# A fused attention and MLP kernel: first loads on one GpSimd queue, a new opening, a halved last tile

## The chip, the cores and the metric

The kernel runs on one core of one Trainium2 chip. The metric is the device time of one launch in microseconds (us), lower is better. Engines are named as in the profile: PE (TensorE matmul), PEld (its weight load), DVE (VectorE), ACT (ScalarE), POOL (GpSimd) and SP (SyncE, which only issues DMAs here).

## The reference

A linear attention with decay over 768 positions (4 batches, 8 heads, head size 64) is followed by an MLP with a "snake" activation. In the reference the attention goes block by block:

```python
intra = np.einsum('bhic,bhjc->bhij', qb, kb) * Dmask[None]
intra = np.einsum('bhij,bhjd->bhid', intra, vb)
inter = np.einsum('bhid,bhde->bhie', qb * lam_pow[None], kv_state)
out[:, :, sl] = intra + inter
kv_state = lam_block[None, :, None, None] * kv_state + np.einsum('bhsd,bhse->bhde', kb_dec, vb)
...
h = x @ w_in                       # x: 3072 x 512, w_in: 512 x 2048
s = np.sin(alpha * h)
g = h + s * s / (alpha + 1e-09)
return (g @ w_out)                 # w_out: 2048 x 512
```

## The kernel before, in words

Work is recorded as a list of operations, each with an engine, a duration that the author assumed, and the buffers that it reads and writes. A planner (`Program.add`) gives every operation a start from these durations; `emit` sorts by start and adds the semaphore waits. So the order on each engine follows from the order of recording and from the assumed durations, and each engine executes its list strictly in that order. DMAs that convert float32 to bf16 (k, q, w_in as `w1`, w_out as `w2`) are issued by POOL, plain ones (v in float32, and the output) by SP.

**Attention.** A *step* s is half of a load block: load block d is 128 positions of a pair of batches with all eight heads, brought in by two DMAs each of k, q and v (one per batch of the pair, `u`), and step 2d takes heads 0 to 3, step 2d+1 heads 4 to 7. A step has three parts, all in `sec`: `t` transposes q and k (32 small PE transposes, then one copy `qkT` out of PSUM by DVE or ACT), `s` forms the scores (`S_m`: 16 PE matmuls and one DVE multiplication with the mask), and `o` forms output and state (PE reads `S_m`, the scaled `v2`, `qkT` and the state `Zs`; DVE scales the result into `xT`, and the state goes on through `Zacc` and `Zs`). `prep_v` multiplies v by its decay before `o` may use it.

**MLP.** Chunk c is 512 tokens, the output of steps 4c to 4c+3. `grp_A(c, m)` is one of 16 groups of four 128x512 matmuls with `w1` (then a sine on ACT, a square on POOL, ACT or DVE, and one DVE operation into `gT`). `grp_B(c, s4, m4)` is a quarter of the 16 matmuls with `w2` for output tile s4. The six chunks go through A, then B, and the attention steps of the next chunk stand between the B groups (`B0_SEC`, `SEC1`, `SEC`). A of a chunk needs all four of its steps.

**Loads at the start.** Steps 0 to 3 (load blocks 0 and 1) come before A of chunk 0; load blocks 2 and 3 (steps 4 to 7) must be there during B of chunk 0. Four w2 blocks of four `m` each and the v loads hang together by gates: v of load block 2 may be issued by SP only when the second w2 block has landed, v of block 3 only when the third has:

```python
ISSUE_A0 = {0: lambda: w2_next(0), 2: lambda: load(2, "k"), 4: lambda: load(2, "q"), 6: lambda: w2_next(1),
            8: lambda: load(2, "v", after=[gates[1]]), 9: lambda: load(3, "k"), 12: lambda: load(3, "q"),
            14: lambda: w2_next(2)}
```

Of the kernel before, what the change touches and what calls it, by code (L numbers as in the profile page):

```python
# [27 lines left out]
class Program:  # L28
# [57 lines left out]
    def add(self, eng, fn, dur, reads=(), writes=(), slot=None, nbytes=0, after=()):  # L86
# [20 lines left out]
        op.start = self.place(eng, max(t, self.issued[eng]), self.ISSUE[eng])  # L107
# [79 lines left out]
def bass_lightning_attn__then__act_snake_kernel(  # L187
# [31 lines left out]
    with es:  # L219
# [77 lines left out]
        def load(d, x, after=(), us=(0, 1)):  # L297
            pair, n = d // NB, d % NB
            r = d % RL
            src, dst = {"k": (k, k2), "q": (q, q2), "v": (v, v32)}[x]  # L300
            for u in us:
                a = bass.AP(src.tensor, (2 * pair + u) * H * S * D + n * BL * D, [[2 * D, 64], [S * D, H], [1, 2 * D]])
                op = rec("SP" if x == "v" else "POOL", lambda e, u=u, a=a: e.dma_start(dst[r][half(u), :, :], a), 0,  # L303
                         writes=[f"{x}.{r}.{u}"], slot=f"{x}{r}", nbytes=262144 if x == "v" else 131072, after=after)
            return op

        def consts():
# [26 lines left out]
        def consts3():  # L334
# [66 lines left out]
        def prep_v(s, engs=("POOL", "DVE")):  # L401
# [4 lines left out]
            reads, writes = [f"v.{r}.0", f"v.{r}.1", "Lv"], [f"v2.{c}"]  # L406
# [9 lines left out]
        def part_keys(x, s):  # L416
            return [f"{x}.{s // 2 % RL}.{u}" for u in range(2)]
        def sec(t=None, o=None, s=None, tb=None, sb_=S_BK, ob=O_BK, peek=False, t_engs=("DVE", "ACT"), via=None):
# [125 lines left out]
            if s is not None:  # L544
# [10 lines left out]
            if has_Z:  # L555
# [3 lines left out]
                if no == 0 and o > 1:  # L559
                    rec("ACT", lambda e: e.copy(zs, z), 0.37, reads=keys_o, writes=[f"Zs.{o % 3}"])  # L560
            if o is not None:
                x, col = (o // 4) % NX, 256 * (no % 2)
                xo = xT[x][:, 2 * ho:2 * ho + 2, col:col + 256].rearrange("p a (u i) -> p u a i", u=2)
                xi = PS[:, ob:ob + 2, 0:256].rearrange("p u (a i) -> p u a i", a=2)
                X_b = bass.AP(Xt, (2 * ho * NB + no) * 128, [[HS * NB * 128, 128], [0, 2], [NB * 128, 2], [1, 128]])
                rec("DVE", lambda e: e.tensor_tensor(xo, xi, X_b, ALU.mult), 0.72,  # L566
                    reads=keys_o + [f"X.{2 * ho + a}.{no}" for a in range(2)],
                    writes=[f"x.{x}.{o % 4}"])
            if o in (0, 1):
                rec("ACT", lambda e: e.copy(zs, z), 0.37, reads=keys_o, writes=[f"Zs.{o % 3}"])  # L570
            if has_Z:
                if no == 0:
                    rec("ACT", lambda e: e.copy(acc[:, :, :], z), 0.4, reads=keys_o, writes=[f"Zacc.{ho}"])
                else:
# [3 lines left out]
                        reads=[f"Zacc.{ho}"], writes=[f"Zs.{o % 3}"])  # L578
            if t is not None:
# [106 lines left out]
        prep_v(3, ("DVE",))
        w1_block(8, 8, after=[v1])
        sec(o=2, ob=4)
        sec(o=3, ob=6)
        alpha_ops(0)  # L690
        alpha_ops2()
        decay_table(2, NB)
        sin_table()
# [13 lines left out]
        def steady(i, peek=False):  # L707
# [4 lines left out]
            return sec(t=t, o=o, s=s, tb=(b, b), peek=peek)  # L712

        gates = {}

        def w2_next(j):
            gates[j] = w2_block(4 * j, 4)

        ISSUE_A0 = {0: lambda: w2_next(0), 2: lambda: load(2, "k"), 4: lambda: load(2, "q"), 6: lambda: w2_next(1),
                    8: lambda: load(2, "v", after=[gates[1]]), 9: lambda: load(3, "k"), 12: lambda: load(3, "q"),  # L720
                    14: lambda: w2_next(2)}

        def v_last():
            gates["v"] = load(3, "v", after=[gates[2]])

        def next_kq(d):
            load(d, "k", after=[gates["v"]])
            load(d, "q", after=[gates["v"]])

        ISSUE_B0 = {0: lambda: w2_next(3), 1: v_last, 9: lambda: next_kq(4)}  # L730
        ISSUE_A1 = {0: lambda: load(5, "k"), 3: lambda: load(5, "q"), 8: lambda: ahead(8), 11: lambda: ahead(9),
                    14: lambda: ahead(10)}
        every, low = range(8), range(4)
        B0_SEC = {3: dict(t=4, tb=(6, 7)), 5: dict(t=5, s=4, tb=(6, 6)), 7: dict(t=6, s=5, tb=(7, 7)),
                  9: dict(t=7, s=6, tb=(6, 6)), 10: dict(o=4, s=7, ob=6), 11: dict(o=5, ob=4),
                  12: dict(o=6, ob=6), 13: dict(o=7, t=8, tb=(6, 6), ob=4)}
        SEC = {2: 0, 5: 1, 8: 2, 10: 3}
        SEC1 = {4: 0, 6: 1, 9: 2, 11: 3}
        SQ = {3: "ACT", 6: "DVE", 8: "ACT", 11: "DVE", 13: "ACT"}
        for c in range(NCH):  # L740
            if c == 1:
                load(4, "v")
                load(5, "v")
            for m in range(NM):
                grp_A(c, m, every if m < 12 else range(2, 4) if m == 15 and c else range(4, 8),
                      (SQ.get(m, "POOL"),) if c > 1 else ("POOL", "ACT", "DVE"))
                if c == 0 and m in ISSUE_A0:
                    ISSUE_A0[m]()
                if c == 1 and m in ISSUE_A1:
                    ISSUE_A1[m]()  # L750
                if c == 1 and m == 7 or c > 1 and m in (3, 7, 11):
                    grp_B(c - 1, 3, 3 if c == 1 else m // 4 + 1, low)
            b_seq = [(s4, m4) for m4 in range(4) for s4 in range(2)] + [(2, m4) for m4 in range(4)] + [(3, 0)]
            if c == 0:
                b_seq = [(s4, m4) for m4 in range(2) for s4 in range(4)]
                b_seq += [(s4, m4) for s4 in range(3) for m4 in (2, 3)] + [(3, 2)]
            for i, (s4, m4) in enumerate(b_seq):
                if c == 0 and i in ISSUE_B0:
                    ISSUE_B0[i]()
# [46 lines left out]
```

## Time and profile before

| | |
|---|---|
| median of 3 runs | 239.6 us (239.52 to 240.24) |
| the profiled execution | 239.02 us, of which 237.2 us span |
| PE busy, share of the span | 213.8 us, 90% |
| DVE, ACT, POOL busy | 141.6, 124.1, 112.3 us |
| mean granted TensorE clock | 0.968 of full |
| data moved by the DMA engines | 23.49 MB, mean 99 GB/s |

The span runs from the first to the last instruction on the core; the 1.8 us between it and the device time are launch and end. Busy shares are averages over stages with different limits, so the stages have to be read one by one. The granted clock is the share of full TensorE speed that the chip allowed; full is 2.4 GHz, and 0.50 in a stretch means 1.2 GHz throughout.

### The profile page before, as it was taken

Reading aid. Unit: us, or ns where it says so; the run is one execution under the profiler, and the core shown is the slowest. Engines: PE = TensorE matmul, PEld = TensorE weight load, DVE = VectorE, ACT = ScalarE, POOL = GpSimd, SP = SyncE. Lnnn points to the kernel's source line nnn. Section 1 sums busy time; section 2 is a strip of 40 time slices with the busy share of each in tenths; the row PEclk is TensorE's granted clock in tenths of the full one; section 3 lists DMA queues with packets and bytes.
Section 4 is the critical chain, followed back from the end, with each engine's and each line's share of the span. In section 5 each row is a group of like instructions: output and inputs, shape, how many; then the busy total and the mean of one; then the engine's idle time right before and its main releaser. Section 6 shows DMA issues by size and latency. Waiting matters only on the chain.

```text
span 237.2 us, 6413 instructions
## 1 busy us (share of the span) xinstructions
PE 213.8 (90%) x2817; PEld 108.4 (46%) x2817; DVE 141.6 (60%) x202; ACT 124.1 (52%) x193; POOL 112.3 (47%) x146
## 2 busy tenths in 40 slices
PE   6355999569899999989999999999999999999993
PEld 5253344234444445544455544456444464444441
DVE  2647599043839995737875647865558756378300
ACT  3752599012049963357755367815377631668120
POOL 8568900081173562858554495553275600455300
PEclk9997699958999999999999999999999999999998
DMA  7999999939289990993052990222110203102033
GB/s 67 162 204 154 199 191 194 233 51 89 68 122 184 234 175 5 147 197 57 8 128 22 235 146 3 71 64 68 44 28 0 48 3 91 45 0 47 0 88 88
DMA packets 46283, 23.49 MB, mean 99 GB/s; under 512 B 26784, under 2 KB 42672, under 8 KB 46256
## 3 DMA queue, kind: packets, MB, share of 16 engines
q0 software_dynamic: 29568, 10.49, 38.8%
q1 hardware_dynamic: 16512, 12.59, 22.5%
q8 instruction: 22, 0.36, 0.7%
q14 instruction: 5, 0.04, 0.1%
q10 hardware_dynamic: 176, 0.01, 0.0%
HBM read 27.28 MB, written 6.29 MB: 142 GB/s over the span
## 4 chain that ended last, share of the span: by engine, by line
PE 64%; DMA 14%; DVE 11%; POOL 5%; ACT 3%; issue 1%; SPq 1%; POOLq 0%; ACTq 0%
PE PS L642 28%; PE PS L605 24%; DMA v<-in_v_dram 7%; DMA w<-in_moe_w_out_dram 5%; PE PS L429 4%; DVE S_m L553 4%; DVE gT L619 2%; DMA k<-in_k_dram 2%; PE PS L438 2%; ACT t L609 2%; PE PS L461 2%; PE PS L451 2%; DVE u L617 2%; POOL k L303 1%; DVE xT L566 1%
## 5 line engine op out<-in xcount | busy, mean ns | idle before, releaser
L642 PE MATMUL PS<-w,gT 128*128 128x512 bf16 x384 | 92.0, 385 | 0.0
L605 PE MATMUL PS<-xT,w 128*128 128x512 bf16 x384 | 88.3, 386 | 1.5 <-DVE xT L566 1.5
L619 DVE SCALAR_TENSOR_TENSOR gT<-u,r_sb,PS 128x512 bf16<-128x512 bf16 x96 | 69.6, 746 | 29.4 <-POOL u L617 26.6
L609 ACT ACTIVATE t<-PS,alpha_sb 128x512 bf16<-128x512 f32 x96 | 63.3, 682 | 22.7 <-PE PS L605 22.1
L617 POOL TENSOR_TENSOR u<-t 128x512 bf16<-128x512 bf16 x44 | 44.9, 1039 | 33.0 <-ACT t L609 33.0
L605 PEld LDWEIGHTS PS<-xT,w 128*128 128x128 bf16 x384 | 37.6, 99 | 49.2 <-issue 3.5
L642 PEld LDWEIGHTS PS<-w,gT 128*128 128x128 bf16 x384 | 35.9, 99 | 42.7 <-issue 1.8
L553 DVE TENSOR_TENSOR S_m<-PS,mask 128x1024 bf16<-128x1024 f32 x24 | 29.2, 1223 | 26.2 <-PE PS L438 26.2
L588 ACT COPY qkT<-PS 128x1024 bf16<-128x1024 bf16 x21 | 21.2, 1013 | 43.2 <-PE PS L461 25.2
L408 POOL TENSOR_TENSOR v<-v,Lv 128x512 bf16<-128x512 f32 x18 | 19.9, 1108 | 39.6 <-DMA v<-in_v_dram 27.4
L649 ACT COPY osb<-PS 128x512 f32<-128x512 f32 x24 | 14.1, 586 | 30.3 <-PE PS L642 30.2
L429 PE MATMUL PS<-ident,q 64*64 64x64 bf16 x384 | 14.5, 207 | 12.4 <-DMA q<-in_q_dram 6.5
L429 PEld LDWEIGHTS PS<-ident,q 64*64 64x64 bf16 x384 | 9.8, 115 | 22.9 <-issue 7.9
L566 DVE TENSOR_TENSOR xT<-PS,Xt 128x512 bf16<-128x512 f32 x24 | 16.4, 685 | 6.3 <-PE PS L461 4.4
L303 POOL DMA_DIRECT2D k<-in_k_dram x24 | 17.1, 719 | 6.5 <-PE PS L438 3.0
L577 POOL CAST Zs<-Zacc 128x256 bf16<-128x256 f32 x16 | 6.5, 408 | 27.2 <-DVE Zacc L575 27.2
L616 ACT ACTIVATE u<-t 128x512 bf16<-128x512 bf16 x28 | 17.6, 630 | 1.2
L617 DVE TENSOR_TENSOR u<-t 128x512 bf16<-128x512 bf16 x24 | 15.7, 652 | 3.2 <-ACT t L609 3.2
L451 PE MATMUL PS<-S_m,v 64*64 64x128 bf16 x384 | 14.3, 231 | 2.7 <-POOL v L408 2.5
L303 POOL DMA_DIRECT2D q<-in_q_dram x24 | 16.7, 712 | 0.0
L461 PE MATMUL PS<-qkT,Zs 64*64 64x128 bf16 x160 | 15.5, 229 | 0.4
L429 PE MATMUL PS<-ident,k 64*64 64x64 bf16 x384 | 13.7, 202 | 0.0
(44 smaller groups left out, 112.8 us busy)
## 6 DMA issues: line engine op xcount, KB each, us to landing
v<-in_v_dram SPq DMA_DIRECT2D x24, 256.0 KB, 5.6
out_dram<-osb SPq DMA_DIRECT2D x48, 128.0 KB, 2.6
k<-in_k_dram POOLq DMA_DIRECT2D x24, 128.0 KB, 4.4
q<-in_q_dram POOLq DMA_DIRECT2D x24, 128.0 KB, 5.6
w<-in_moe_w_out_dram POOLq DMA_DIRECT2D x4, 512.0 KB, 13.8
w<-in_moe_w_in_dram POOLq DMA_DIRECT2D x1, 1024.0 KB, 9.9
w<-in_moe_w_in_dram POOLq DMA_DIRECT2D x2, 256.0 KB, 5.8
w<-in_moe_w_in_dram POOLq DMA_DIRECT2D x1, 512.0 KB, 7.8
```

The lines of the kernel that those rows point to most:

```text
L303: op = rec("SP" if x == "v" else "POOL", lambda e, u=u, a=a: e.dma_start(dst[r][half(u), :, :], a), 0, writes=[f"{x}.{r}.{u}"], slot=f"{x} ...
L408: rec(eng, lambda e: e.tensor_tensor(v2[c][:, :, :], src, L_b, ALU.mult), dur, reads=reads, writes=writes)
L429: last = e.transpose(dst, part((q2, k2)[x], t, u, h, tt), ident[half(u), half(u)])
L451: return e.matmul(dst, v2[o % RC][half(u), hid(h, tj), :], S_m[o % RS][half(u), h % 2 ^ u, h // 2, tj, :], start=start, stop=True, skip_gr ...
L461: return e.matmul(dst, Zs[(o - 2) % 3][half(r), u, h // 2, :], qkT[o % RQ][half(r), u, 0, h // 2, :], start=start, stop=True, skip_group_c ...
L553: rec("DVE", lambda e: e.tensor_tensor(s_out, s_in, mask_b, ALU.mult), 1.25, reads=keys_s + ["mask.0", "mask.1"], writes=[f"S_m.{s % RS}"])
L588: rec(eng, lambda e: (e.copy if eng == "ACT" else e.tensor_copy)(to, ti), dur, reads=keys_t, writes=[f"qkT.{j}"])
L605: last = e.matmul(PS[:, i, :], w1[:, kc, 128 * m:128 * (m + 1)], xT[x][:, kc, :], start=(kc == 0), stop=(kc == NKC - 1))
L609: rec("ACT", lambda e: e.activation(t16[tt][:, :], PS[:, i, :], ACTF.Sin, scale=alpha_sb[:, m:m + 1]), 0.7, reads=bk(i) + ["alpha"], write ...
L617: return e.tensor_tensor(u16[tt][:, :], t16[tt][:, :], t16[tt][:, :], ALU.mult)
L619: rec("DVE", lambda e: e.scalar_tensor_tensor(out=gT[g][:, m, :], in0=u16[tt][:, :], scalar=r_sb[:, m:m + 1], in1=PS[:, i, :], op0=ALU.mul ...
L642: last = e.matmul(PS[:, bank, :], gT[g][:, m, 128 * s4:128 * (s4 + 1)], w2[:, m, :], start=(m == 0), stop=(m == NM - 1))
```

## The change

All loads of load blocks 0 to 3, v among them, are issued by POOL, on its one queue. Their order there is: k, q of block 0; k, q of block 1; v of blocks 0 and 1 in quarters (one DMA for each batch and each half of the heads, so that a step waits for its own heads only); w1 in four equal blocks; then w2 and blocks 2 and 3 in turns. The gates are gone. The opening records its parts in another order, all four multiplications of v go to POOL, and step 3's scores go out through ACT (`via`). During B of chunk 0 the groups go tile by tile through three w2 blocks, two of the groups are moved into A of chunk 1, and the `t` part of step 8 moves into B of chunk 1. In later chunks the fourth step stands one B group later and writes `xT` ahead of `S_m` (`x_first`). The last output tile is computed in two halves of 256 columns, copied out by ACT and by DVE, and its last two DMAs are issued by SP and by ACT. The planner's assumed issue time for the quarter loads is 0.6 of the usual one.

```diff
-        def load(d, x, after=(), us=(0, 1)):
+        def load(d, x, after=(), by_step=False, eng=None):
...
+            for h0, h1 in ((0, HS), (HS, H)) if by_step else ((0, H),):
+                for u in range(2):
...
+                    op = rec(eng or ("SP" if x == "v" else "POOL"),
+                             lambda e, u=u, a=a, h0=h0, h1=h1: e.dma_start(dst[r][half(u), h0:h1, :], a), 0,
...
             def part_keys(x, s):
-            return [f"{x}.{s // 2 % RL}.{u}" for u in range(2)]
+            return [f"{x}.{s // 2 % RL}.{u}.{s % 2}" for u in range(2)]
...
+        def last_tile(c, s4, banks):
...
+            for z, eng in ((0, "ACT"), (1, "DVE")):
...
+                        last = e.matmul(PS[:, bank, 0:256], gT[g][:, m, 128 * s4:128 * (s4 + 1)], w2[:, m, cs],
...
+                for t, q_eng in ((0, "SP"), (1, "SP" if z == 0 else "ACT")):
...
-        consts2()
-        v0 = load(0, "v", after=[k0])
-        v1 = load(1, "v", after=[k1])
-        w1_block(0, 2, after=[k1])
-        prep_v(0, ("POOL",))
-        w1_block(2, 2, after=[v0])
-        w1_block(4, 4, after=[v0])
+        ident_op()
         sec(t=0, tb=(0, 1), t_engs=("DVE",))
         sec(t=1, tb=(2, 3), t_engs=("ACT",))
+        consts2()
+        load(0, "v", by_step=True, eng="POOL")
+        load(1, "v", by_step=True, eng="POOL")
+        w1_block(0, 4)
+        identf_op()
...
-        ISSUE_B0 = {0: lambda: w2_next(3), 1: v_last, 9: lambda: next_kq(4)}
+        ISSUE_A0 = {0: [("w", 0)], 2: [("k", 2)], 4: [("q", 2)], 6: [("w", 1)], 9: [("k", 3)], 12: [("q", 3)]}
+        ISSUE_B0 = {0: [("v", 2), ("w", 2)], 2: [("v", 3), ("w", 3)], 8: [("k", 4)], 10: [("q", 4)]}
+        LAST_B0 = {1: (2, 3), 3: (3, 3)}
...
-                b_seq = [(s4, m4) for m4 in range(2) for s4 in range(4)]
-                b_seq += [(s4, m4) for s4 in range(3) for m4 in (2, 3)] + [(3, 2)]
+                b_seq = [(s4, m4) for m4 in range(3) for s4 in range(4)] + [(0, 3), (1, 3)]
```

**Place 1: POOL in the opening.** The names are buffers (`v_0<-in_v_dram` loads v of block 0; `w<-in_moe_w_in_dram` loads w1; a `TENSOR_TENSOR v_..<-v_..,Lv` is `prep_v`). This is POOL's list before, from the constants on:

```order
L314 AFFINE_SELECT ident<-maskf 128x128
L335 IOTA X_i 128x128
L337 IOTA N_i 128x6
L338 IOTA E_i 128x96
L340 AFFINE_SELECT identf<-maskf 16x16
L303 DMA k_1<-in_k_dram 64x8x128 x2
L303 DMA q_1<-in_q_dram 64x8x128 x2
L325 AFFINE_SELECT mask_0<-maskf 128x256
L325 AFFINE_SELECT mask_1<-maskf 128x256
L393 DMA w<-in_moe_w_in_dram 128x4x256 [waits s_d_k1]
L408 TENSOR_TENSOR v_0<-v_0,Lv 128x512 [waits s_d_v0,s_ACT]
L393 DMA w<-in_moe_w_in_dram 128x4x256
```

The same place of POOL's list after the change:

```order
L309 DMA q_1<-in_q_dram 64x8x128 x2
L316 AFFINE_SELECT ident<-maskf 128x128 [waits s_DVE]
L335 AFFINE_SELECT mask_0<-maskf 128x256
L335 AFFINE_SELECT mask_1<-maskf 128x256
L309 DMA v_0<-in_v_dram 64x4x128 x4
L309 DMA v_1<-in_v_dram 64x4x128 x4
L408 DMA w<-in_moe_w_in_dram 128x4x512
L353 AFFINE_SELECT identf<-maskf 16x16
L423 TENSOR_TENSOR v_0<-v_0,Lv 128x512 [waits s_ACT,s_d_v00p]
L423 TENSOR_TENSOR v_1<-v_0,Lv 128x512 [waits s_d_v04p]
L423 TENSOR_TENSOR v_2<-v_1,Lv 128x512 [waits s_d_v10p]
L423 TENSOR_TENSOR v_3<-v_1,Lv 128x512 [waits s_d_v14p]
```

The selections for `ident` and `identf` now stand behind the k and q loads of block 1; eight quarter loads of v and the first w1 load are issued ahead of four multiplications in a row, of which two were DVE's before.

**Place 2: the loads of blocks 2 and 3.** Before, v stands on SP, behind semaphores of k and of w2 blocks (`w2_4` is the second, `w2_8` the third); this is the head of SP's list:

```order
L303 DMA v_0<-in_v_dram 64x8x128 [waits s_d_k0]
L303 DMA v_0<-in_v_dram 64x8x128
L303 DMA v_1<-in_v_dram 64x8x128 [waits s_d_k1]
L303 DMA v_1<-in_v_dram 64x8x128
L303 DMA v_2<-in_v_dram 64x8x128 [waits s_d_w2_4]
L303 DMA v_2<-in_v_dram 64x8x128
L303 DMA v_3<-in_v_dram 64x8x128 [waits s_d_w2_8]
L303 DMA v_3<-in_v_dram 64x8x128
```

After, POOL's list has them between the w2 loads, and the multiplications of v follow behind the loads of blocks 4 and 5 (shown as buffers 0 and 1):

```order
L309 DMA q_3<-in_q_dram 64x8x128 x2
L309 DMA v_2<-in_v_dram 64x8x128 x2
L413 DMA w<-in_moe_w_out_dram 128x4x512
L309 DMA v_3<-in_v_dram 64x8x128 x2
L413 DMA w<-in_moe_w_out_dram 128x4x512
L309 DMA k_0<-in_k_dram 64x8x128 x2
L309 DMA q_0<-in_q_dram 64x8x128 x2
L309 DMA k_1<-in_k_dram 64x8x128 x2
L309 DMA q_1<-in_q_dram 64x8x128 x2
L423 TENSOR_TENSOR v_4<-v_2,Lv 128x512 [waits s_d_v2p]
L423 TENSOR_TENSOR v_0<-v_2,Lv 128x512
L423 TENSOR_TENSOR v_1<-v_3,Lv 128x512 [waits s_d_v3p]
```

The v loads have no wait of their own any more; what holds them is only their place in POOL's list.

## Rows read from the trace of the kernel before

**Rows 1.** The head of the profile's page: busy us (share of the span) of each engine.

```profile
PE 213.8 (90%) x2817; PEld 108.4 (46%) x2817; DVE 141.6 (60%) x202; ACT 124.1 (52%) x193; POOL 112.3 (47%) x146
```

**Rows 2.** Windows by stage: start:end length, busy (instructions) per engine, PEclk, DMA, GB/s.

```profile
0.00:23.00 23.00, 11.67 (x369) 10.06 (x369) 12.58 (x21) 11.92 (x23) 15.93 (x29) 0.95 1.07 145
23.00:39.10 16.10, 16.06 (x64) 6.76 (x65) 12.22 (x22) 12.74 (x21) 7.07 (x12) 0.87 1.40 193
39.10:69.20 30.10, 24.09 (x446) 12.20 (x445) 14.00 (x21) 6.71 (x10) 9.12 (x13) 0.89 0.73 115
103.50:136.90 33.40, 33.12 (x465) 16.56 (x466) 21.43 (x29) 19.93 (x31) 18.99 (x22) 1.00 0.60 102
```

**Rows 3.** Chain of waits, 37 to 70 us: start, length, what.

```profile
25.17 12.51 DMA w<-in_moe_w_out_dram
...
38.33 9.66 DMA v<-in_v_dram
48.02 0.69 DVE v L408
48.71 0.61 DVE qkT L588
...
51.13 3.53 PE PS L642 x8
...
55.78 1.83 PE PS L642 x8
57.62 0.40 PE PS L429 x16
...
58.06 0.35 PE PS L429 x10
```

**Rows 4.** Waits of PE, 39 to 70 us: total, times, longest.

```profile
PE PS L429 <- DVE qkT L588: 4.4, 1, 4.4
```

**Rows 5.** Windows of the stretches in which the granted clock changes.

```profile
20.00:26.80 6.80, 6.01 (x90) 3.08 (x79) 3.69 (x8) 1.01 (x3) 6.67 (x12) 0.54 1.05 171
...
49.40:54.10 4.70, 4.63 (x56) 2.33 (x56) 1.23 (x1) 1.01 (x1) 4.66 (x7) 0.50 0.60 56
54.10:69.20 15.10, 13.56 (x335) 7.31 (x334) 8.79 (x13) 3.79 (x5) 3.12 (x7) 0.98 0.56 77
```

**Rows 6.** Timeline of the opening: start, length, instruction, idle before and its releaser.

```profile
5.33 1.41 POOL L303 DMA_DIRECT2D k<-in_k_dram  x2
...
7.78 0.44 PE L429 MATMUL PS<-ident,q 64*64 64x64 bf16 x16 [3.01 <-DMA q<-in_q_dram]
...
8.05 0.86 POOL L325 TENSOR_SCALAR_AFFINE_SELECT mask<-maskf 128x256 bf16<-128x256 f32 x2
...
14.07 0.44 PE L429 MATMUL PS<-ident,q 64*64 64x64 bf16 x16 [3.45 <-DMA q<-in_q_dram]
...
18.70 1.04 POOL L408 TENSOR_TENSOR v<-v,Lv 128x512 bf16<-128x512 f32 x1 [2.19 <-DMA v<-in_v_dram]
...
19.50 0.78 DVE L408 TENSOR_TENSOR v<-v,Lv 128x512 bf16<-128x512 f32 x1
...
23.04 7.24 PE L605 MATMUL PS<-xT,w 128*128 128x512 bf16 x23 [0.66 <-DVE xT L566]
```

**Rows 7.** Windows in which mostly k and q, then w2, then v alone were moved.

```profile
29.00:31.00 2.00, 2.00 (x11) 0.91 (x10) 1.68 (x4) 1.97 (x4) 1.20 (x2) 1.00 1.45 190
...
38.00:41.00 3.00, 3.00 (x15) 1.29 (x14) 2.93 (x6) 2.94 (x5) 0.00 (x0) 1.00 1.38 201
...
45.00:46.00 1.00, 0.00 (x0) 0.00 (x0) 0.00 (x0) 0.00 (x0) 0.00 (x0) 1.00 1.15 234
```

**Rows 8.** Timeline of the end.

```profile
233.26 0.59 ACT L649 COPY osb<-PS 128x512 f32<-128x512 f32 x1 [2.81 <-PE PS L642]
233.87 1.11 SPq L655 DMA_DIRECT2D out_dram<-osb  x2
```

**Rows 9.** DMA issues, 225 to 238 us: count, size, us to landing.

```profile
out_dram<-osb SPq DMA_DIRECT2D x8, 128.0 KB, 2.4
```

More of the change, by code (lines that the diff above doesn't have):

```diff
@@ L106, in add @@
         op.kslot = self.slots[slot]
-        op.start = self.place(eng, max(t, self.issued[eng]), self.ISSUE[eng])
+        issue = self.ISSUE[eng] * (0.6 if 10000 < nbytes < 100000 and eng == "POOL" else 1)
+        op.start = self.place(eng, max(t, self.issued[eng]), issue)
         self.issued[eng] = op.start
@@ L416, in part_keys, with sec @@
         def part_keys(x, s):
-            return [f"{x}.{s // 2 % RL}.{u}" for u in range(2)]
-        def sec(t=None, o=None, s=None, tb=None, sb_=S_BK, ob=O_BK, peek=False, t_engs=("DVE", "ACT"), via=None):
+            return [f"{x}.{s // 2 % RL}.{u}.{s % 2}" for u in range(2)]
+        def sec(t=None, o=None, s=None, tb=None, sb_=S_BK, ob=O_BK, peek=False, t_engs=("DVE", "ACT"), via=False, x_first=False, z_late=None, later=False):
             po, no, ho = where(o) if o is not None else (0, 0, 0)
@@ L569, in sec, with put_x @@
[L569 to L574, printed above, removed]
+                def put_x():
+                    x, col = (o // 4) % NX, 256 * (no % 2)
+                    xo = xT[x][:, 2 * ho:2 * ho + 2, col:col + 256].rearrange("p a (u i) -> p u a i", u=2)
+                    xi = PS[:, ob:ob + 2, 0:256].rearrange("p u (a i) -> p u a i", a=2)
+                    X_b = bass.AP(Xt, (2 * ho * NB + no) * 128, [[HS * NB * 128, 128], [0, 2], [NB * 128, 2], [1, 128]])
+                    rec("DVE", lambda e: e.tensor_tensor(xo, xi, X_b, ALU.mult), 0.72,
+                        reads=keys_o + [f"X.{2 * ho + a}.{no}" for a in range(2)],
+                        writes=[f"x.{x}.{o % 4}"])
@@ new lines, in first_state @@
+                def first_state():
+                    rec("ACT", lambda e: e.copy(acc[:, :, :], z), 0.4, reads=keys_o, writes=[f"Zacc.{ho}"])
+                if part != 1 and (no > 0 or o == 0):
+                    put_x()
+                if has_Z and no == 0:
+                    rec("ACT", lambda e: e.copy(zs, z), 0.37, reads=keys_o, writes=[f"Zs.{o % 3}"])
+                if no == 0 and o > 0:
+                    put_x()
+                if part == 0:
+                    return
+                if has_Z and no == 0:
+                    if z_late is None:
+                        first_state()
+                    else:
+                        z_late.append(first_state)
+                elif has_Z:
@@ L578, in sec @@
                         reads=[f"Zacc.{ho}"], writes=[f"Zs.{o % 3}"])
+            puts = [put_S] if s is not None else []
+            if o is not None:
+                puts.insert(0 if x_first else 1, put_O)
+            if later:
+                return put_O if o is not None else put_S
+            for put in puts:
+                put()
             if t is not None:
@@ L683, in bass_lightning_attn__then__act_snake_kernel @@
         sec(s=2, sb_=0)
-        sec(s=3, sb_=2)
+        zl = []
+        s3 = sec(s=3, sb_=2, via=True, later=True)
+        sec(o=0, ob=4, z_late=zl)
+        s3()
         prep_v(2, ("POOL",))
[L686 to L690, printed above, removed]
+        prep_v(3, ("POOL",))
+        sec(o=1, ob=6, z_late=zl)
+        w1_block(4, 4)
+        w1_block(8, 4)
+        w1_block(12, 4)
+        o2 = sec(o=2, ob=0, later=True)
@@ L691, in bass_lightning_attn__then__act_snake_kernel @@
+        o3 = sec(o=3, ob=2, later=True)
+        for f in o2, o3:
+            f(0)
+        for f in zl:
+            f()
+        sin_table()
+        alpha_ops(4)
+        for f in o2, o3:
+            f(1)
         alpha_ops2()
-        decay_table(2, NB)
-        sin_table()
         nl, npr = [6], [8]
```

137 lines of the change are left out of this document (74 added, 63 removed).

## The prediction

> **What bounds the kernel now.** I read the head of the page first: PE is busy for 90% of the span of 237.2 us [rows 1]. An average over stages says little, so next the windows by stage [rows 2]. In the middle (103.5 to 136.9 us, one whole chunk) PE is busy for 33.12 of 33.40 us at full clock: there PE is the bound and only less PE work could help. The first 69 us are different. The opening lasts 23.0 us with PE busy for 11.67; A of chunk 0 lasts 16.1 us at a mean clock of 0.87; B of chunk 0 lasts 30.1 us with PE busy for 24.09, at 0.89. What waits last in the opening and in B0 is thus what the change can touch.
>
> In B0 the chain of waits [rows 3] tells the story in order: a w2 load in flight for 12.51 us from 25.17, then a v load for 9.66 us from 38.33 to 48.0 (its issue was held by the gate until that w2 block landed), then DVE multiplying v. DVE's list had a copy `qkT` queued behind that multiplication, and PE needs the copy: PE waits 4.4 us for it, once [rows 4]. Right behind the wait the granted clock is 0.50 from 49.4 to 54.1 [rows 5]; eight B matmuls take 3.53 us there against 1.83 us a little later [rows 3]. So one gate on v costs 4.4 us of standing still and then about half of 4.7 us of slow running. In the remainder of B0, 54.1 to 69.2, PE lacks 15.10 - 13.56 = 1.54 us [rows 5].
>
> In the opening [rows 6] PE waits 3.45 us for q of block 1 until 14.07 (k and q shared the DMA engines with v from SP), POOL and DVE multiply v of block 1 at 18.70 and 19.50, until 20.28, and A starts at 23.04: 2.76 us later.
>
> **The change, part by part.** *Prices.* A k or q load (128 KB) at 190 GB/s takes 0.69 us of the DMA engines, a w block of four (512 KB) at 201 GB/s 2.6 us, a v load (256 KB) at 234 GB/s 1.12 us when SP issues it [rows 7]. The trace has no v load on POOL's queue. It reads as many bytes as a k load does, so 0.69 us is the lower end; 1.12 us from its own row is the nearest above. I take 0.9 us.
>
> *Issue time.* POOL issues two k loads in 1.41 us, 0.70 each [rows 6]; a w block names as many pieces of memory (512), so I give it the same. A quarter load of v names half as many: from 0.35 us (cost by pieces) to 0.70 (cost by DMA). I take 0.50, in between, because nothing in the trace separates them. The two k loads at 5.33 were issued while DVE was preparing constants, and took no longer than 0.70 each. The Trainium skill, "SBUF — State Buffer", section "Who interferes with whom", says that a DVE copy in a two-port mode and GpSimd exclude each other for the whole instruction, and that descriptors for DMAs of GpSimd wait for it. By that rule DVE's two `qkT` copies of 0.61 us each [rows 3] would fall into the stretch of the eight quarters and hold POOL for 1.2 us, and the sum would be 229.5 instead of 228.3; no row here shows such a hold.
>
> *Opening.* Selections worth a few tenths go behind k and q of block 1, so q1 is issued by 7.9 (before 6.70 + 1.39 = 8.1), and nothing of v shares the engines: q of block 0 was there at 7.78, and four loads of 0.69 to 0.8 us behind it land at about 11.0 instead of 14.07 [rows 6]. POOL then makes `ident` and the masks, to 9.1 (before to 8.91), issues eight quarters, 4.0 us, to 13.1, the w1 load to 13.8, and `identf`, to 14.1. Four multiplications of 1.04 us follow: 18.3 (bounds by the issue time: 17.1 and 19.9). They do not wait for data: v of block 0 needs q1's end at about 10 plus two quarters' transfer and a microsecond to land, under 13.5. PE takes step 2 while step 3's v is multiplied, so behind the last multiplication stand one `o` part and one DVE scaling: 2.3 us instead of 2.76. A starts at 20.6 (19.4 to 22.2), 2.4 us earlier. Three w1 blocks are issued only after the multiplications, from 18.3 on; the second one lands at about 23, while A's fifth group starts no sooner than 20.6 + 4 x 0.9 = 24.2. The cover there is 1.2 us.
>
> *A of chunk 0.* The same 64 matmuls. 20.0 to 26.8 ran at 0.54 [rows 5], so 3.8 us of this stage were at half speed, a loss of 1.9 us. PE is denser in the new opening, but I can't read the new grant from this trace: all full would give 14.2 us, a whole 6.8 us at half 17.6. I leave 16.1. B0 starts at 36.7 instead of 39.1.
>
> *B of chunk 0.* I lay the loads end to end: v of blocks 0 and 1 and the first w1 block end at 16.2; a gap until 19.6 because POOL is multiplying; three w1 blocks to 27.4; then w2, k2 q2 (four loads) to 32.8; w2 35.4; k3 q3 38.2; v2 40.0; w2 42.6; v3 44.4; w2 47.0; each is usable about a microsecond later. PE needs them later: a group is 1.83/2 = 0.9 us [rows 3], so the second w2 block is wanted at 40.6 (there at 36.4), v2 for step 4 at about 47.5 (there at 41, multiplied by 42.7), the third w2 block at 47.5 (43.6), v3 at 52 (45.4), the fourth at 53.5 (48). The cover is 4 us or more everywhere. So the 4.4 us wait goes, and with it the reason for the half clock: half of 4.7 us is 2.35. Of the lacking 1.54 us I give back half, 0.8, since no `qkT` copy stands behind a v multiplication any more. One group (0.9) and the `t` part of step 8 (0.40 + 0.35 [rows 3]) merely move into chunk 1: 1.65 us leaves B0 and comes back. B0 = 30.1 - 4.4 - 2.35 - 0.8 - 1.65 = 20.9 us, and A of chunk 1 starts at 57.6 instead of 69.2.
>
> *Later chunks.* PE lacks 0.28 us in the whole chunk read above [rows 2]; `x_first` and the step moved by one group can win or lose a few tenths. I take nothing.
>
> *The end.* The last copy takes 0.59 us and two DMAs 1.11 us to issue, one after the other, with 2.4 us to landing [rows 8, 9]. Half the columns for the last copy: between 0.3 and 0.59 us; SP and ACT issue side by side: half of 1.11 saved. PE's columns are the same. I take 0.8 us off (0.5 to 1.1).
>
> *Sum.* 69.2 - 57.6 = 11.6, less 1.65 that comes back, plus 0.8: 10.75 us. From the profiled execution's own 239.02 us that gives 228.3. The median of the runs shown is 0.6 us above that execution; I leave the forecast at 228.3, well inside the range.
>
> **Rivals.** *The clock is full from A0 on:* 1.9 us of A0 comes back as well, and the rest of the lacking time: 225.5. For it: PE waits less in the opening. Against: four `o` parts still wait for POOL's multiplications.
>
> *The opening gives its gain back:* quarters cost 0.70 us each to issue and the multiplications, now all on POOL, come later. A starts at 22.8: 228.3 + 2.2 = 230.5. For it: POOL has 4 us more of issue and two more multiplications. Against: it was idle for 2.19 us in the same stretch [rows 6].
>
> *Loads still late in B0:* if v on this queue takes 2.0 us a load, 1.1 more than I took, the eight v loads in front of the last w2 block put it off by 8.8 us, of which 5.5 are covered (53.5 less 48): 3.3 us lost, 231.6. Against: no row for v is above 1.12 us.
>
> *Not faster:* POOL is the only issuer and executes in order; whatever slows one load holds every load and every multiplication behind it. With a v load of 0.9 + x us the loss is 8x - 5.5 by the step above (A0 itself moves by less: four loads stand in front of it, and the last quarter has 2 us to spare before its multiplication). The gain of 10.75 is used up at x = 2.0, a v load of 2.9 us; at 3.1 us the time would be 228.3 + 12.1 = 240.4. The nearest row is 1.12 us [rows 7], so I give it little.
>
> *The change does not do what it says,* because a wait of POOL (state copies and `aeps` stand before the first w2 load) holds the loads until PE stands still as before and the clock drops again: 4.4 + 2.35 come back and leave 235.
>
> **How the numbers follow.** Chances: forecast 0.45; full clock 0.18; opening gives back 0.17; loads late 0.09; stall comes back 0.06; not faster 0.05. The 0.05 splits into 0.015 within 0.3% and 0.035 slower; 0.3% is about what a measurement of this kernel can tell from no change. The range reaches down past the full clock with the early A0 (19.4, 1.2 us) and up past late loads: 223.5 to 233.0, and leaves out about 2 in 10.
>
> **What would show it.** Right: PE has no wait over 1 us between 36 and 58 us; A0 starts near 20.6, B0 near 36.7, A1 near 57.6; the granted clock stays 1.00 after B0 starts; the last DMAs are issued side by side. Wrong: POOL's quarter issues near 0.7 us each, v loads above 1.2 us, B groups that wait for w2, or a half clock inside B0. The first thing that would break the forecast is a B0 that waits again, for loads now queued behind each other on POOL.

## The result, and the profile after

The changed kernel took 230.18 us (median of 4 runs, 228.26 to 232.99), the kernel before, measured beside it, 239.92 us (239.52 to 241.62): a ratio of 0.9554 with a 95% interval of 0.9452 to 0.9657. Medians and ranges here and below are of all runs, while the ratios leave out slow runs, which lie more than 1.5% above the fastest of their kernel. The forecast was 228.3, the range 223.5 to 233.0: the direction and the range held, and the gain was 9.7 us where 10.75 were forecast. The profiled execution was the slowest of the four (232.99 us, span 230.7), so I read a second profile of the same kernel beside it (231.46 us, span 229.4), called the second profile below. Where they differ I say which.

The head of the page, against [rows 1]: busy us (share of the span) of each engine.

```profile
PE 213.6 (93%) x2833; PEld 110.1 (48%) x2833; DVE 140.8 (61%) x201; ACT 125.3 (54%) x194; POOL 122.4 (53%) x160
```

PE has the same work (213.8 before) in 6.5 us less span. The windows by stage, against [rows 2]: opening, A of chunk 0, B of chunk 0, and everything from A of chunk 1 to the last B matmul (the third window ends 0.14 us into the fourth).

```profile
0.00:23.10 23.10, 12.80 (x369) 10.73 (x369) 11.89 (x19) 12.19 (x23) 20.08 (x35) 0.68 0.90 133
23.10:39.75 16.65, 16.64 (x65) 6.99 (x66) 12.53 (x23) 12.48 (x21) 16.17 (x25) 0.83 1.40 190
39.75:63.10 23.35, 20.64 (x410) 10.72 (x409) 13.07 (x19) 5.86 (x8) 9.02 (x13) 1.00 1.15 159
62.96:227.58 164.62, 163.62 (x1993) 81.77 (x1992) 103.00 (x142) 94.78 (x143) 77.12 (x88) 1.00 0.43 81
```

The same of the second profile:

```profile
0.00:21.48 21.48, 12.82 (x369) 10.83 (x369) 13.09 (x19) 11.90 (x22) 19.61 (x35) 1.00 0.93 132
21.48:38.07 16.59, 16.58 (x64) 7.00 (x65) 12.54 (x23) 12.69 (x23) 16.10 (x25) 1.00 1.37 194
38.07:61.57 23.50, 20.51 (x409) 10.62 (x408) 12.88 (x19) 5.80 (x8) 9.04 (x13) 1.00 1.27 166
61.57:226.22 164.65, 163.56 (x1993) 81.93 (x1992) 103.26 (x142) 94.75 (x143) 77.14 (x88) 1.00 0.44 81
```

A stretch for which the trace holds no clock record counts as 1.00. The records of the second profile begin at 27.12 us, so the clock of its first two rows is not a reading; those of the kernel before begin at 17.10 us, so the 0.95 of its opening in [rows 2] is not one either.

B0 fell from 30.10 us to 23.35 and 23.50, at a granted clock of 1.00 instead of 0.89, but PE is still idle for 2.7 to 3.0 us of it. What it waits for is in the waits of PE up to 75 us of the first profile (total, times, longest):

```profile
PE PS L444 <- POOL ident L316: 3.3, 1, 3.3
PE PS L489 <- issue: 3.2, 2, 1.7
PE PS L444 <- DMA q<-in_q_dram: 1.9, 1, 1.9
...
PE PS L444 <- issue: 0.4, 1, 0.4
```

The 4.4 us wait for `qkT` [rows 4] is gone. New is "issue": time in which PE waits for nothing that the profile shows, 3.2 us in two stops. The chain of waits shows where the one in B0 lies (start, length, what), in the place of [rows 3]:

```profile
53.26 1.24 DVE S_m L568
54.54 0.42 PE PS L466 x16
55.06 1.70 issue
56.77 0.35 PE PS L489 x12
...
57.46 1.83 PE PS L677 x8
```

The timeline of the opening, against [rows 6]:

```profile
8.02 0.33 PE L444 MATMUL PS<-ident,q 64*64 64x64 bf16 x16 [3.26 <-POOL ident L316]
...
8.62 4.99 POOL L309 DMA_DIRECT2D v<-in_v_dram  x8
...
11.98 0.44 PE L444 MATMUL PS<-ident,q 64*64 64x64 bf16 x16 [1.89 <-DMA q<-in_q_dram]
...
14.47 4.50 POOL L423 TENSOR_TENSOR v<-v,Lv 128x512 bf16<-128x512 f32 x4
...
21.30 0.26 PE L489 MATMUL PS<-v,k 64*64 64x64 bf16 x1 [1.48 <-issue]
...
23.11 1.46 PE L640 MATMUL PS<-xT,w 128*128 128x512 bf16 x3 [0.58 <-DVE xT L581]
```

q of block 1 now reaches PE at 11.98 instead of 14.07, and POOL is done multiplying at 18.97, but in this execution PE then stops for 1.48 us inside an `o` part. The second profile has no such stop there and starts A at 21.48.

### The profile page after: what moved, and what is told of

Read it like the earlier page. It is cut to its first block, busy times and chain, and to the rows that moved or that the text cites. A ratio compares the mean times of both kernels' runs of the same rounds, so it can differ in the third digit from the quotient of the medians.

```text
span 230.7 us, 6459 instructions
## 1 busy us (share of the span) xinstructions
PE 213.6 (93%) x2833; PEld 110.1 (48%) x2833; DVE 140.8 (61%) x201; ACT 125.3 (54%) x194; POOL 122.4 (53%) x160
## 4 chain that ended last, share of the span: by engine, by line
PE 82%; DVE 7%; POOL 6%; issue 3%; ACT 1%; POOLq 0%
PE PS L640 34%; PE PS L677 33%; PE PS L444 5%; DVE gT L654 3%; PE PS L466 3%; PE PS L476 3%; PE PS L453 2%; POOL v L309 2%; PE PS L704 2%; PE PS L489 1%; DVE u L652 1%; POOL k L309 1%; POOL q L309 1%; DVE S_m L568 1%; DVE xT L581 1%
## 5 line engine op out<-in xcount | busy, mean ns | idle before, releaser
L677 PE MATMUL PS<-w,gT 128*128 128x512 bf16 x368 | 87.4, 380 | 0.2 <-issue 0.2
L652 POOL TENSOR_TENSOR u<-t 128x512 bf16<-128x512 bf16 x44 | 45.4, 1051 | 31.8 <-ACT t L644 31.7
L677 PEld LDWEIGHTS PS<-w,gT 128*128 128x128 bf16 x368 | 33.8, 98 | 39.6
L568 DVE TENSOR_TENSOR S_m<-PS,mask 128x1024 bf16<-128x1024 f32 x23 | 28.0, 1222 | 23.4 <-PE PS L453 23.4
L423 POOL TENSOR_TENSOR v<-v,Lv 128x512 bf16<-128x512 f32 x20 | 21.4, 1083 | 28.7 <-DMA v<-in_v_dram 14.6
L684 ACT COPY osb<-PS 128x512 f32<-128x512 f32 x23 | 13.5, 585 | 31.6 <-PE PS L677 31.6
L652 DVE TENSOR_TENSOR u<-t 128x512 bf16<-128x512 bf16 x24 | 14.1, 588 | 3.5 <-ACT t L644 3.5
L489 PE MATMUL PS<-v,k 64*64 64x64 bf16 x320 | 11.4, 205 | 3.2 <-issue 3.2
## 6 DMA issues: line engine op xcount, KB each, us to landing
v<-in_v_dram POOLq DMA_DIRECT2D x4, 256.0 KB, 12.7
```

What stands on the lines that cost most here:

```text
L423: rec(eng, lambda e: e.tensor_tensor(v2[c][:, :, :], src, L_b, ALU.mult), dur, reads=reads, writes=writes)
L568: rec("DVE", lambda e: e.tensor_tensor(s_out, s_in, mask_b, ALU.mult), 1.25, reads=keys_s + ["mask.0", "mask.1"], writes=[f"S_m.{s % RS}"])
L652: return e.tensor_tensor(u16[tt][:, :], t16[tt][:, :], t16[tt][:, :], ALU.mult)
L677: last = e.matmul(PS[:, bank, :], gT[g][:, m, 128 * s4:128 * (s4 + 1)], w2[:, m, :], start=(m == 0), stop=(m == NM - 1))
```

## The experiments

### What the stall in B of chunk 0 was made of

My theory was the prediction's: a gated v load holds DVE's multiplication, that holds the copy `qkT` behind it in DVE's list, and PE stands still and then runs at half clock. Three kernels break this chain at different links and leave PE's order in B0 as it was; a fourth has the new tail alone.

**v of blocks 2 and 3 on POOL's queue, in turns with w2, gates gone** (left out are a few lines on the load's arguments, and the end of the gate on k and q of block 4):

```diff
-                    8: lambda: load(2, "v", after=[gates[1]]), 9: lambda: load(3, "k"), 12: lambda: load(3, "q"),
-                    14: lambda: w2_next(2)}
+                    9: lambda: load(3, "k"), 12: lambda: load(3, "q")}
...
+        def v_w2(d, j):
+            load(d, "v", eng="POOL")
+            w2_next(j)
...
-        ISSUE_B0 = {0: lambda: w2_next(3), 1: v_last, 9: lambda: next_kq(4)}
+        ISSUE_B0 = {0: lambda: v_w2(2, 2), 2: lambda: v_w2(3, 3), 9: lambda: next_kq(4)}
```

> The kernel before, with only the loads of blocks 2 and 3 changed: v of these blocks on POOL's queue, in turns with the last two w2 blocks, no gates; opening, order on PE and the end stay as before. Theory: B of chunk 0 loses the 4.4 us wait and the half clock behind it (2.35 us), so about 232.9 us against 239.6. Rival: the loads were late because the DMA engines were full, and PE only waits elsewhere: above 237.

**The gates alone gone, v still issued by SP:**

```diff
-                    8: lambda: load(2, "v", after=[gates[1]]), 9: lambda: load(3, "k"), 12: lambda: load(3, "q"),
+                    8: lambda: load(2, "v"), 9: lambda: load(3, "k"), 12: lambda: load(3, "q"),
...
-            gates["v"] = load(3, "v", after=[gates[2]])
+            gates["v"] = load(3, "v")
```

> The kernel before, with only the gates on v of blocks 2 and 3 taken away; v stays on SP, so it is issued at about 13 us, ahead of most of w1. Theory (the gate made the wait, the queue does not matter): the 4.4 us wait and the half clock go, 6.75 us; four v loads of 1.1 us now stand in front of the later w1 blocks, which may cost A of chunk 0 up to 2 us: 233 to 235. Rival (it takes POOL's queue and its order): 237 or more, because w1 or w2 comes late instead.

**The loads as before, all multiplications of v in B0 on POOL:**

```diff
-                    prep_v(i)
+                    prep_v(i, ("POOL",))
```

> The kernel before, gates and queues untouched; only the four multiplications of v for steps 4 to 7 all go to POOL, so DVE's copy of qkT no longer stands behind a v multiplication. Theory (the wait comes from DVE's list, not from v being late for its own user): PE goes on with transposes, scores and B groups until about 52 us, v is multiplied by 49.4, the 4.4 us wait goes and with it the half clock: 233 to 234. Rival (v itself is what PE needs next): less than 1 us gained, 238.6 or more.

**The halved last tile alone** (the new `last_tile` put into the kernel before):

```diff
-        for m4 in range(1, 4):
-            grp_B(NCH - 1, 3, m4, low)
+        last_tile(NCH - 1, 3, low)
```

> The kernel before, with only the last output tile in two halves of 256 columns, copied by ACT and DVE, last DMAs on SP and ACT. Theory: half of 1.11 us of issue and part of the last copy saved, 0.8 us (0.5 to 1.1): 238.8. Rival: 32 weight loads instead of 16 and the landing time eat it: no difference.

Measured together, with 239.44 us for the kernel before (13 runs):

| kernel | median us (range) | ratio, 95% |
|---|---|---|
| v on POOL, in turns with w2 | 233.39 (232.82 to 234.53) | 0.9724 [0.9668, 0.978] |
| gates alone gone | 233.54 (231.6 to 236.66) | 0.9724 [0.9639, 0.981] |
| multiplications on POOL | 234.68 (232.11 to 236.18) | 0.9736 [0.9656, 0.9816] |
| halved last tile | 239.32 (237.89 to 240.45) | 0.9978 [0.9939, 1.0016] |

B0 in windows (start:end length, busy per engine, then PEclk): of v on POOL, of the gates gone, of the multiplications on POOL, and of the tail alone, each the one row for B0 of its kernel.

```profile
42.34:65.03 22.69, 20.73 (x440) 11.44 (x446) 14.23 (x20) 7.70 (x11) 5.33 (x9) 1.00 1.08 159
```
```profile
39.34:62.20 22.86, 20.75 (x440) 11.44 (x446) 12.78 (x19) 7.34 (x10) 3.24 (x7) 1.00 0.91 127
```
```profile
42.34:65.40 23.06, 20.95 (x440) 11.51 (x446) 12.27 (x18) 7.71 (x11) 10.72 (x16) 1.00 0.90 145
```
```profile
41.11:70.77 29.66, 23.36 (x440) 12.57 (x446) 14.07 (x21) 6.70 (x10) 9.31 (x14) 0.88 0.74 116
```

These windows end 0.4 us into A of chunk 1; up to its first matmul B0 is 22.3, 22.4 and 22.6 us in the first three. Any one of the three links taken away brings B0 from 30.1 to 22.7 to 23.1 us, and the half clock goes with the wait; the fourth kernel, which keeps the chain, keeps both. This is its wait of PE:

```profile
PE PS L429 <- DVE qkT L588: 3.3, 1, 3.3
```

As whole kernels all three are faster, but the intervals of the second and third reach 0.981 and 0.982, so for them a gain under 2% is not excluded. The third kernel says most. Its DVE and POOL timelines:

```profile
46.42 0.69 DVE L588 COPY qkT<-PS 128x1024 bf16<-128x1024 bf16 x1 [1.37 <-PE PS L429]
```
```profile
50.27 4.04 POOL L408 TENSOR_TENSOR v<-v,Lv 128x512 bf16<-128x512 f32 x4 [17.84 <-DMA v<-in_v_dram]
```

Here v is multiplied at 50.27, later than the 48.02 of [rows 3], and PE still does not wait: its waits between 40 and 75 us hold nothing over 0.2 us at a time. So PE did not need v yet. It needed the copy that stood behind v in DVE's list. The queue is not what counts either: on POOL's queue or on SP's, without the gate the time is the same (233.39 and 233.54 us).

The tail alone is not resolved by its ten runs (0.1 us in the medians).

### The opening, part by part

The changed kernel once more, and three edits of it, measured together with 239.51 us for the kernel before (11 runs).

> The changed kernel once more, for a second profile and more times beside its variants. Theory (the forecast's sum holds when PE's instruction supply does not stall): 228 to 229 us, A of chunk 0 from about 21.5 to 23. Rival: the first profile is typical, 231 to 233 us.

**Without the 32 idle matmuls:**

```diff
         consts()
-        idle_pe(32)
```

> The changed kernel without the 32 idle matmuls at the start (they compute nothing that is used). Theory: PE's two stops of 1.48 and 1.70 us with nothing to wait for come at the end of a portion of its instruction stream whose next portion arrives late; 32 matmuls fewer move both ends 32 matmuls on in the program, the first one into A of chunk 0, where PE uses up instructions slowly, so that stop goes: A of chunk 0 starts about 1.5 us earlier and the time falls by 1 to 1.5 us. Rival: the stops belong to the place in the program (a wait that the profile does not show): they stay at the same matmul and the time does not fall.

**v of blocks 0 and 1 in four loads instead of eight:**

```diff
-        load(0, "v", by_step=True, eng="POOL")
-        load(1, "v", by_step=True, eng="POOL")
+        load(0, "v", eng="POOL")
+        load(1, "v", eng="POOL")
```

> The changed kernel with v of blocks 0 and 1 in four loads of 256 KB instead of eight quarters. Theory: the eight quarters cost POOL 4.99 us of issue and four loads about 3.0, but the data then pace the multiplications (256 KB at about 1.1 us each, first one usable later): within 0.7 us of the changed kernel. Rival: issue time is what bounds the opening, then 1.5 to 2 us faster.

**Two of the four multiplications back on DVE:**

```diff
-        prep_v(1, ("POOL",))
+        prep_v(1, ("DVE",))
...
-        prep_v(3, ("POOL",))
+        prep_v(3, ("DVE",))
```

> The changed kernel with two of the four multiplications of the opening (steps 1 and 3) back on DVE. Theory: the row of four on POOL (14.5 to 19.0 us) paces the opening; two of them on DVE bring the last one and the three w1 loads behind them forward by up to 2 us, and A of chunk 0 by 1 to 2 us: 1 us faster. Rival: DVE is full there with scores and scaling, and nothing is gained or up to 1 us lost.

| kernel | median us (range) | ratio, 95% |
|---|---|---|
| the changed kernel again | 231.14 (228.73 to 232.7) | 0.9618 [0.9563, 0.9673] |
| no idle matmuls | 229.31 (227.31 to 229.91) | 0.9578 [0.9537, 0.9619] |
| four loads of v | 232.19 (230.17 to 233.41) | 0.9723 [0.9683, 0.9763] |
| two multiplications on DVE | 231.67 (230.59 to 233.22) | 0.9695 [0.9656, 0.9734] |

The changed kernel itself gave the rival's time, not the 228 to 229 us of the theory. Neither other form of the opening is shown to be better. The four loads lie about 1 us behind in the medians, with ranges that overlap. The timeline of POOL with four loads shows the trade:

```profile
8.62 2.79 POOL L309 DMA_DIRECT2D v<-in_v_dram  x4
...
14.99 2.04 POOL L423 TENSOR_TENSOR v<-v,Lv 128x512 bf16<-128x512 f32 x2 [2.66 <-DMA v<-in_v_dram]
17.57 2.49 POOL L423 TENSOR_TENSOR v<-v,Lv 128x512 bf16<-128x512 f32 x2 [0.54 <-DMA v<-in_v_dram]
```

The issue is 2.20 us shorter, but now POOL waits 2.66 us for the first whole load; with quarters it did not wait for data at all. Per DMA the issue is 0.70 us for a whole load (2.79/4) and 0.62 for a quarter (4.99/8): half the pieces save a tenth, so the cost is almost by DMA.

Without the idle matmuls the median is 1.8 us lower, but the intervals overlap. I ran that kernel again, beside 239.46 us for the kernel before (11 runs):

> The changed kernel without the 32 idle matmuls (they compute nothing that is used), a second time, on whatever chip comes. Theory: the stops of PE depend on where a count of its instructions falls, so this version again stands 1 to 2 us below the changed kernel's 231.1: a ratio to the kernel before of about 0.957. Rival: its lead was scatter between executions, and the ratio is that of the changed kernel or worse, 0.962 to 0.967.

It gave 230.39 us (228.53 to 233.26), 0.9629 [0.9588, 0.9671], the ratio of the changed kernel itself. So the lead is not shown, and I have no version that is shown to beat the changed kernel. The 1.70 us stop did go, though: neither profile without the idle matmuls has it, and PE's longest stop for its own instructions up to 75 us lies elsewhere and is shorter (one row of PE's waits from each of the two). The rival that a stop belongs to its place in the program is contradicted by that.

```profile
PE PS L453 <- issue: 0.9, 1, 0.9
```
```profile
PE PS L453 <- issue: 1.0, 1, 1.0
```

### Where the stops of PE come from

Both profiles of the changed kernel stop for 1.70 us at the same place, behind 729 matmuls. The page lists a queue "instruction" (q8) of 22 packets and 0.36 MB, 16 KB each. I infer that it brings PE's program: 0.36 MB over PE's 5,666 matmuls and weight loads is 64 bytes for each, and the stops below lie behind its packets. One packet starts at 54.45, in the slice of this view that jumps to 779 GB/s (the DMA view of the first profile, 54.2 to 55.2 us, in 40 slices), behind 705 matmuls, while the loads keep the engines at 9 tenths:

```profile
DMA  9999999999999999999999999999999999999999
GB/s 184 184 164 195 184 195 184 174 184 184 779 174 164 174 164 174 174 174 154 164 154 164 143 164 154 184 143 144 133 144 143 143 154 174 133 133 154 164 133 123
...
q8 instruction: 1, 0.02, 6.1%
```

PE runs dry 24 matmuls later, at 55.06, and goes on at 56.77. The 1.48 us stop in the opening of the first profile has its packet too: it starts at 18.91, 23 matmuls ahead, when the engines had just run nearly empty (31 GB/s from 18.5 to 19.5 us), and PE goes on at 21.30. So PE goes on 2.3 to 2.4 us after the packet's start whether the engines are full or not; what can be late is the start. Theory: the portion comes late because k and q of blocks 4 and 5 fill the engines. So I let those loads wait for groups of chunk 1, first alone, then with the idle matmuls gone as well.

```diff
-        ISSUE_B0 = {0: [("v", 2), ("w", 2)], 2: [("v", 3), ("w", 3)], 8: [("k", 4)], 10: [("q", 4)]}
-        ISSUE_A1 = {0: [("v", 4)], 1: [("k", 5)], 3: [("q", 5)], 4: [("v", 5)]}
+        ISSUE_B0 = {0: [("v", 2), ("w", 2)], 2: [("v", 3), ("w", 3)]}
+        ISSUE_A1 = {0: [("v", 4), ("k", 4)], 1: [("q", 4)], 3: [("k", 5)], 4: [("v", 5), ("q", 5)]}
...
-                    loads(*(ISSUE_A0, ISSUE_A1)[c].get(m, ()))
+                    loads(*(ISSUE_A0, ISSUE_A1)[c].get(m, ()), after=[a_op] if c == 1 else [])
```

> The changed kernel with k and q of load blocks 4 and 5 issued only from A of chunk 1 on (each waits for an A group), so that no loads run from about 51 to 57 us; order on PE unchanged. Theory (a portion of PE's instructions arrives late when it has to get past a full queue of loads): the stop of 1.70 us before matmul 729, seen in four profiles of this opening, goes, and the time falls by about 1.5 us to 229.5. Rival (the stop depends on the count of instructions alone, not on the loads): it stays, and the time stays at 231.

> The same late loads, and no idle matmuls at the start (they compute nothing that is used). Theory: with either edit the stop at matmul 729 is gone, so the two together win no more than the idle matmuls' removal did: 229 us. Rival: they win separately, 227.5.

**Both edits, and v of the opening on SP behind k of block 1,** so that POOL is free to issue all of w1 early:

```diff
-        load(0, "v", by_step=True, eng="POOL")
-        load(1, "v", by_step=True, eng="POOL")
+        load(0, "v", by_step=True, after=[k1])
+        load(1, "v", by_step=True, after=[k1])
```

> As before, and the eight quarter loads of v of blocks 0 and 1 are issued by SP, waiting for k of block 1 to land, while POOL issues all w1 loads and the first w2 load right behind the masks. Theory (POOL's 5 us of issue is what holds its multiplications until 14.5): they start when the first quarter lands, between 13 and 14, A of chunk 0 starts about 1 us earlier and w1 is there long before: 228. Rival (v then shares the DMA engines with w1 and q): the multiplications start later than 14.5, and the time is 229 to 232.

| kernel (the kernel before beside them: 240.53 us, 11 runs) | median us (range) | ratio, 95% |
|---|---|---|
| late k, q of blocks 4, 5 | 231.87 (228.68 to 234.13) | 0.9573 [0.9514, 0.9632] |
| those, and no idle matmuls | 232.71 (230.4 to 234.54) | 0.9656 [0.9607, 0.9704] |
| those two, and v on SP | 244.11 (241.52 to 246.57) | 1.0125 [1.0069, 1.018] |

With the late loads the stop is gone from B0, which is 2.1 us shorter than in the second profile (window of B0, then PE's waits between 40 and 75 us):

```profile
38.07:59.42 21.35, 20.31 (x409) 10.60 (x408) 12.68 (x19) 5.69 (x8) 4.68 (x6) 1.00 0.71 120
```
```profile
PE PS L444 <- issue: 0.4, 1, 0.4
PE PS L466 <- DVE S_m L568: 0.3, 1, 0.3
```

But it is given back where the moved loads now lie. PE's waits between 75 and 105 us of the same kernel:

```profile
PE PS L444 <- issue: 2.4, 2, 2.1
PE PS L677 <- issue: 1.3, 1, 1.3
```

From A of chunk 1 to the last B matmul this execution takes 169.5 us (164.65 in the second profile), with the clock at 0.50 from 88.6 to 92.0. In the total nothing is won that the scatter would show, and the sum with the other edit is none. The stop follows the loads, as the theory says: the fifth packet, which started at 54.46 behind 705 matmuls, now starts at 49.78 behind 642, and PE's new stops end 2.4 us after packets at 85.02 and 97.21. That loads hold back the start of a fetch stays an inference: I have no run with the loads in place and the fetch early.

The last kernel, 11.4 us above the one without this edit, tells what it costs to let w1 and v come side by side. POOL's multiplications there (timeline):

```profile
20.11 1.04 POOL L425 TENSOR_TENSOR v<-v,Lv 128x512 bf16<-128x512 f32 x1 [7.54 <-DMA v<-in_v_dram]
23.76 1.04 POOL L425 TENSOR_TENSOR v<-v,Lv 128x512 bf16<-128x512 f32 x1 [2.61 <-DMA v<-in_v_dram]
...
31.14 1.04 POOL L425 TENSOR_TENSOR v<-v,Lv 128x512 bf16<-128x512 f32 x1 [2.60 <-DMA v<-in_v_dram]
```

Beside a POOL queue that holds all of w1 and a w2 block, quarters of v on another queue take a median of 10.9 us to land (3.1 in the changed kernel), and A starts at 34.57. From 16 to 28 us POOL's queue (q0) and SP's (q1) move the same number of packets, and SP's hold half the bytes (the DMA view of these 12 us; queue: packets, MB, share of the engines):

```profile
q0 software_dynamic: 1728, 1.72, 84.4%
q1 hardware_dynamic: 1735, 0.84, 34.9%
```

So v gets a third of the bytes while w1 and w2 pass. What an early issue of w1 could win is lost many times over. SP's packets of v hold 512 bytes here, those of v on POOL's queue in the changed kernel 4,096; how much of the loss is this, and how much the order of w1 and v, no run here separates.

## Why the prediction was right, and where it was off

In us, by its own steps (the rest after A1 is read up to the end of the span):

| step | before | forecast | first profile | second |
|---|---|---|---|---|
| A0 starts | 23.04 | 20.6 | 23.11 | 21.48 |
| A0 | 16.1 | 16.1 | 16.63 | 16.59 |
| B0 | 30.1 | 20.9 | 23.2 | 23.5 |
| A1 to the last B matmul | 164.1 | 165.75 | 164.6 | 164.65 |
| from there to the end | 4.0 | 3.2 | 3.1 | 3.2 |

*B0, the stall.* Right in mechanism and in size. 30.1 less 4.4, 2.35 and 0.8 is 22.55; the three kernels that change only this gave 22.7 to 23.1, and each is about 5 to 6 us faster as a whole. (In the profiles of two of them the opening, which they leave as it was, took 3.0 and 4.2 us longer than in [rows 6].) The clock is 1.00 through B0 in all of them. The covers held too, though v landed 3 to 4 us later than laid out (41 and 45.4). POOL's timeline:

```profile
44.05 2.04 POOL L423 TENSOR_TENSOR v<-v,Lv 128x512 bf16<-128x512 f32 x2 [2.62 <-DMA v<-in_v_dram]
49.12 1.04 POOL L423 TENSOR_TENSOR v<-v,Lv 128x512 bf16<-128x512 f32 x1 [3.02 <-DMA v<-in_v_dram]
```

Between these two landings lie a w2 block (2.6 us [rows 7]) and the two loads of v of block 3, so a v load on POOL's queue took about 1.2 us, not the 0.9 that I chose. No long wait of PE follows.

*B0, the rest.* Mis-sized: 20.9 forecast, 23.2 and 23.5 measured. 1.70 and 0.41 us in the first profile (1.70 and 0.68 in the second) are stops for PE's own instructions, which no term of the sum held. With the stop moved away B0 is 21.35. The forecast's own sign, no wait of PE over 1 us between 36 and 58 us, failed by this 1.70; for data PE had no such wait.

*The opening.* I forecast 20.6 within 19.4 to 22.2; the second profile's 21.48 lies inside, the first's 23.11 does not. The issue of a quarter cost 0.62 us where I took 0.50; begun a little earlier than laid out, the multiplications end at 18.97 (18.50 in the second profile) instead of 18.3. From there to A I took 2.3 us: it was 3.0 in the second profile, and 2.7 in the first besides the 1.48 us stop for instructions. Why it is longer no run here shows. The prediction's alternative by the Trainium skill, "SBUF — State Buffer", section "Who interferes with whom", did not come: the section's rule is for DVE copies in a two-port mode, whose conditions the prediction did not check for these copies out of PSUM. In the trace the issues follow each other every 0.61 to 0.63 us, those that meet DVE's copies at 8.7 and 12.7 within 0.02 us of the others. The old opening, moreover, is not always as in the profile of before: the four kernels of the first table all keep it, and three of them started A at 25.56, 26.03 and 27.24, with q of block 1 at PE at 15.8 to 17.0 instead of 14.07. The new one started A at 21.4 to 23.1 in all eight profiles that load v by POOL there. Some of the 9.7 us between the medians, where the profiled executions differ by only 6.0 and 7.6, may be this; no run here shows it, and none has the new opening alone. That the median came within 2 us of the forecast is thus in part luck: the two profiled executions lie 3.2 and 4.7 us above it.

*A of chunk 0.* "I leave 16.1" was near (16.6), the rival of a full clock did not come: half speed lasts for 5.6 to 5.7 us of A0 in both profiles, where the prediction took 3.8 (in the second it shows in the pace of the matmuls, see the last section). Executions do differ here: over all profiles of the study A0 took 14.87 to 16.65 us.

*Later chunks.* I took nothing; it was a gain of 1.1 us. PE's waits after A1 of the kernel before hold this row, which has no counterpart after the change, where `x_first` puts `xT` ahead of `S_m` (the kernel with v on POOL alone, which has the old order, keeps the row):

```profile
PE PS L605 <- DVE xT L566: 0.8, 1, 0.8
```

*The tail.* 4.0 to 3.1 us, forecast 0.8 less. The timeline shows the two queues side by side as forecast:

```profile
226.27 2.27 SPq L712 DMA_DIRECT2D out_dram<-osb  x3
...
227.62 0.42 DVE L708 COPY osb<-PS 128x256 f32<-128x256 f32 x1 [10.76 <-PE PS L704]
228.08 0.54 ACTq L712 DMA_DIRECT2D out_dram<-osb  x1
```

As a whole-kernel time it lies below what ten runs tell apart.

*The rivals.* Late loads, the stall coming back and "not faster" did not happen. "The opening gives its gain back" happened in one profile of the two, and for another reason than the one I gave it.

## What to carry to other kernels

When PE waits for a small copy, look at what stands ahead of that copy in its engine's list: an instruction whose data isn't needed yet can stall the core for a load that nobody wants, and moving it to an idle engine is worth as much as an earlier load. Where the DMA engines are full, a load that is wanted first belongs ahead of the others: beside them, on a second queue, v got a third of the bytes and came late, while v of blocks 2 and 3, issued early, came in time from either queue. Before forecasting a gain on PE, look for the "issue" stops and count PE's instructions: if the reading above is right, a fetch of its program that starts late adds a term of 1 to 2 us that no wait in the trace of before shows.

## What the runs showed of the hardware that I had not expected

If the reading above is right, PE's program comes in 22 fetches of 16 KB, and one that starts only 24 matmuls ahead of need stopped PE for 1.70 us (other stops were of 1.3 to 2.1 us): PE went on 2.3 to 2.4 us after the packet's start, with the engines full or nearly empty.

Two load queues that both have work moved equal numbers of packets (1,728 and 1,735 in 12 us), so the one with packets of half the size moved half the bytes.

A page can show a full clock where PE runs at half pace, because no record counts as full. The second profile has 1.00 here, but no clock record before 27.12 us, and its first 5.7 us of A0 hold as many matmuls as the same stretch of the first profile does at a recorded 0.50, half as many as later (the last row is the next 5.7 us of the second profile):

```profile
23.10:28.80 5.70, 5.69 (x14) 2.09 (x15) 2.71 (x6) 2.36 (x4) 5.22 (x9) 0.50 1.24 204
```
```profile
21.50:27.20 5.70, 5.70 (x14) 2.08 (x15) 2.72 (x6) 2.51 (x6) 5.23 (x9) 1.00 1.24 206
27.20:32.90 5.70, 5.70 (x29) 2.55 (x26) 4.76 (x9) 5.14 (x10) 5.70 (x10) 1.00 1.36 186
```

So I read the pace from matmuls of one shape, 128x512, per stretch, and not from the clock column alone, above all near the start of a trace.
